# Fetching the slot lists and rows of all four early expert units during the fourth MLP block

## Chip, cores and metric

The kernel runs on one core of one Trainium2 chip. The metric is the device time of one execution in microseconds (us), lower is better; the number to predict is the median of several executions of the changed kernel. PE is TensorE, DVE is VectorE, ACT is ScalarE, POOL is GpSimd and SP is SyncE, which here only issues DMAs.

## What is computed

```python
attn = softmax((q @ k_m.T) / sqrt(64)) @ v_m      # k_m, v_m pooled by softmax(phi) over the sequence
x = elu(attn_out @ w_in) @ w_out                  # 2304 tokens, 512 -> 2048 -> 512
noisy = x @ w_gate + log1p(exp(x @ w_noise)) * noise
top2 = the two largest of the 8 experts for each token, with softmax weights top2_w
for e in range(8):
    for k in range(2):
        mask = top2[:, k] == e
        out[mask] += top2_w[mask, k, None] * (relu(x[mask] @ w1[e]) @ w2[e])   # 512 -> 1024 -> 512
```

## The kernel before

The work is one list of **units**, and each unit is a loop over slices of its hidden width (line 863 flattens both into iterations `i`). Units 0 to 3 are the four MLP blocks of 4, 5, 4 and 5 token tiles of 128, with 16 iterations each. Units 4 to 15 are experts, with 8 iterations each. Units 4 to 7 are the **early** units: the first 256 slots (two tiles) of experts 0 to 3, filled from the tokens of blocks 0 and 1 alone, so that they can run before the last block's tokens are routed. Units 8 to 11 are the other three tiles of the same experts, and units 12 to 15 are the other four experts with five tiles.

In an iteration PE runs `layer1` of its own slice (line 729) and `layer2` of the slice two iterations earlier (lines 775 to 777). ACT and DVE split fp32 weights into a high and a low part for iteration `i + 2` (lines 462 and 468), from a raw tile of 1 MB that serves two iterations; three raw tiles rotate (line 387), and each load (line 395) is issued seven iterations before its first slice, when its tile has just been freed.

An expert unit's tokens reach it in these steps:

- `gating(b)` runs after block `b` and ends in indirect scatters by POOL (line 634) that write each token's number and weight into its expert's slots of the DRAM table `lst`.
- `fetch(n)` reads the unit's slots of `lst` into the tile `ids` by a DMA on SP's queue (line 688), and then POOL gathers the rows, one tile `xg` of 128 rows by each indirect DMA (line 693). The gathers of early units read only rows of blocks 0 and 1 (line 685).
- `spread(n)` transposes each gathered tile on PE (line 704) and splits the result into `xh` and `xl` on ACT and DVE (lines 134 and 135). A unit's `spread` is queued when the unit ahead of it begins, and must be through when its own begins (`drain`, line 876).
- At a unit's end `put_rows` scales the accumulators and POOL adds them to `out` (line 797).

All engines take their instructions in the order in which the program was written down, so a waiting instruction holds everything behind it on its engine or queue. That order is set by two queues of generators, `heads` and `tails`, which `tick` advances at two or three places of every iteration. A generator that yields "next" goes on in the next iteration at the earliest. `fetch` yields four of these behind its gathers, so what stands behind it in `tails` comes four iterations later. Since `lst` is tracked as one DRAM tensor, a list read that stands behind a `gating`'s scatters in the program waits until they have landed.

Of the kernel before, what the change touches and what calls it, by code (L numbers as in the profile page):

```python
# [40 lines left out]
def moe_stack_kernel(ctx, tc, phi, kv, q, wmlp, wgn, noise, wmoe, out):  # L41
# [73 lines left out]
    def att_loads(b):  # L115
        return ([lambda: load_phi(b)] + [lambda w=w, c=c: load_kv(b, w, c) for w in range(2) for c in range(2)]
                + [lambda h=h: load_q(b, h) for h in range(2)])
# [9 lines left out]
    def settle():  # L127
        for f in deferred:
            f()
        deferred.clear()  # L130
# [277 lines left out]
    def fold(b, j, g):  # L408

        if g == 0:  # L410
            folds[b, j] = [fp.tile([P, 2, 512], F32R, tag=n, name=n) for n in ("fh", "fl")]
        bk = side_bank()
        for jj in range(2):
            pe.matmul(bk[64 * jj:64 * jj + 64], att["vT", b][:, g, 64 * jj:64 * jj + 64],
                      raws["a", 16 * b + 4 * j + 2 * g + jj], start=True, stop=True, tile_position=(0, 64 * jj))
        later(lambda: halve(bk, *(t[:, g] for t in folds[b, j])))
# [55 lines left out]
    heads, tails, moe = [], [], {}  # L472
    wants, stepped = {}, {}

    def step_on(gen):
        place[0] = ""
        wants[id(gen)] = next(gen)
# [28 lines left out]
    def drain(gen):  # L506
        place[0] = ""
        for queue in (heads, tails):
            while gen in queue:
                try:  # L510
                    next(queue[0])
                except StopIteration:
                    wants.pop(id(queue.pop(0)), None)
# [163 lines left out]
        yield  # L677


    def fetch(n, wait=0):  # L680

        for _ in range(wait):
            yield "next"
        mp = moe["pool"]
        rows = JUNK + (BLOCKS[2][0] * P if n["early"] else N)
        ids = mp.tile([P, 5, 2], I32, tag="ids", name="ids", bufs=6)
        a, nt = n["e"] * N + n["s0"], n["nt"]
        sp.dma_start(ids[:, :nt], lst[a:a + nt * P].rearrange("(t p) c -> p t c", p=P))
        n["ids"] = ids
        n["xg"] = []  # L690
        for tt in range(nt):
            xg = mp.tile([P, DM], F32, tag="xg", name="xg", bufs=12)
            pool.indirect_dma_start(out=xg, out_offset=None, in_=x2d[:rows],
                                    in_offset=bass.IndirectOffsetOnAxis(ap=ids[:, tt, 0:1], axis=0))
            n["xg"].append(xg)
        for _ in range(4):
            yield "next"

    def spread(n):
        xt = n["x"]  # L700
        for tt in range(n["nt"]):
            bk = side_bank()
            for c in range(4):
                pe.transpose(bk[:, c * P:(c + 1) * P], n["xg"][tt][:, c * P:(c + 1) * P], ident)
            v = bk.rearrange("p (c n) -> p c n", c=4)
            hi = xt[0][:, :, tt * P:(tt + 1) * P]
            later(lambda a=(v, hi, xt[1][:, :, tt * P:(tt + 1) * P]): halve(*a))
            yield

    def new_x():  # L710
        return [moe["pool"].tile([P, 4, 640], F32R, tag=n, name=n, bufs=2) for n in ("xh", "xl")]

    def splits(u):
        if u["kind"] == "mlp":
            return [(0, S // 2), (S // 2, S // 2)]
        n = u["nt"] * P
        return [(0, n)] if n <= 512 else [(0, n // 2), (n // 2, n // 2)]
# [41 lines left out]
    def hidden_c():  # L759
        for m, gh, gl, o in low:  # L760
            dve.tensor_tensor(gl[:, o], m, gh[:, o].bitcast(F32), op=OP.subtract)
        low.clear()
# [71 lines left out]
    k = NE * TPE + 1  # L834
# [4 lines left out]
    units = [dict(kind="mlp", blk=k, nt=BLOCKS[k][1], nf=16) for k in range(4)]  # L839
# [4 lines left out]
    late = 4 + NA  # L844
# [22 lines left out]
    for i in range(len(flat)):  # L867

        near = [flat[j][0]["nt"] for j in (i - LAG, i - LAG + 1) if 0 <= j < len(flat)]
        banks["tags"] = ["px"] + ["acc%d" % t for t in range(max(near, default=0), 5)]  # L870
        if i < len(flat):
            u, f = flat[i]
            k = units.index(u)
            if f == 0:
                if "need" in u:
                    drain(u["need"])
                if k == 1:
                    paced += zeros
                if k == 4:
                    moe["pair"] = True  # L880
                if k == 3:
                    side_stack.close()
                    moe["pool"] = ctx.enter_context(tc.tile_pool(name="moe", bufs=1))
                if k >= 3 and k + 1 < len(units):
                    n = units[k + 1]
                    n["x"] = new_x()
                    n["need"] = spread(n)
                    if k == 3:
                        tails += [fetch(n, 3), n["need"], fetch(units[5])]
                    else:  # L890
                        (heads if k + 1 in (late, late + 1) else tails).append(n["need"])
                        if k == late:
                            tails.append(overflow_table())
                        if k + 2 < len(units) and k + 2 not in (late, late + 1):
                            tails.append(fetch(units[k + 2]))
            if k in (1, 2) and f == 0:
                paced = att_loads(k + 1) + paced
            if k < 3 and f == 0:
                n = units[k + 1]
                n["need"] = attention(k + 1)  # L900
                heads.append(n["need"])
            if k and u["kind"] == "mlp" and f == 0:
                u["x"] = att["x", k]
            j = (i + 2) // 4
            turn_ = u["kind"] == "mlp" and f % 4 > 1 and j < 16
            if turn_:
                while ("vT", j // 4) not in att:
                    step_on(heads[0])
                place[0] = ""
                fold(j // 4, j % 4, f % 4 - 2)  # L910
            tick("", turn_)
            hidden_c()
            mine = [(h, c) for h, c in (("a", i + 5), ("b", i)) if c < NRAW]
            conv1_lo(mine)
            conv2(mine)
            nxt = []
            if u["kind"] == "mlp":
                nxt += [("b", i)] * (i >= NRAW)
            if 64 <= i + 2 < len(chunks):
                nxt += [("a", i + 2), ("b", i + 2)]  # L920
            prep_hi(nxt)
            gh = gp.tile([P, 640], F32R, tag="gh", name="gh")
            gl = gp.tile([P, 640], F32R, tag="gl", name="gl")
            cuts = splits(u)
            if u["kind"] == "mlp":
                elu, parts = ep.tile([P, 2, S], F32, tag="elu", name="elu"), []
            for j, (s0, n) in enumerate(cuts):
                ph = layer1(u, i, s0, n)
                if j == len(cuts) - 1:
                    tick("mid")  # L930
                o = slice(s0, s0 + n)
                if u["kind"] == "mlp":
                    elu_a(elu, ph, o)
                    parts.append((ph, o))
                else:
                    relu_(ph, gh, gl, o)
            settle()
            prep_lo(nxt)
            keep(mine)
            conv1_hi([(h, c) for h, c in (("a", i + 6), ("b", i + 1)) if c < NRAW])  # L940
            for n in at_end.get(i, []):
                load_to(n)
            for _ in range(2 if f < 10 else 1):
                if paced:
                    paced.pop(0)()
            if u["kind"] == "mlp":
                elu_b(u, f, elu, parts, gh, gl)
            tick("late")
            pend.append((u, f, i, gh, gl))
        else:  # L950
            tick()
        if i >= LAG and i < len(flat) - 1:
            pu, pf, pi, pgh, pgl = pend.pop(0)
            layer2(pu, pf, pi, pgh, pgl)
            if pf == pu["nf"] - 1:
                for t in range(pu["nt"]):
                    put_rows(pu, t, pu["acc"][t])
                if pu["kind"] == "mlp":
                    b = pu["blk"]
                    if b < 2:  # L960
                        tails.append(gating(b, pu["rows"]))
                    else:
                        heads.append(gating(b, pu["rows"]))
                    if b == 3:
                        heads += [fetch(units[late]), fetch(units[late + 1])]
# [70 lines left out]
```

## Time and profile before

| what | value |
|---|---|
| median of 3 executions | 962.58 us (962.42 to 963.52) |
| the profiled execution's own time | 955.79 us |
| its span in the profile | 954.0 us |
| PE busy / PE weight load busy | 898.1 us (94%) / 738.6 us (77%) |
| DVE, ACT, POOL busy | 549.6 us (58%), 452.1 us (47%), 173.5 us (18%) |
| mean granted clock of PE | 0.98 |
| moved by DMA | 153.11 MB, mean 160 GB/s |

Times in the trace count from the start of the span. The profiled execution is one sample beside the three that were timed; it is 6.79 us below their median. PE is the engine that is nearly always busy, so what matters of any other engine is whether PE has to wait for it. Block 3 ends at about 455 us, and the early units run their first layer from about 444 us to about 570 us: unit 4 from 444.7, unit 6 from 517.7 and unit 7 from 542.7 us.

### The profile page before, as it was taken

The numbers are of one execution on the slowest core, as the hardware profiler recorded it, in microseconds if no ns is written. First come the engines' busy times: TensorE is split into PE (matmuls) and PEld (weight loads), VectorE is DVE, ScalarE is ACT, GpSimd is POOL, SyncE is SP. The second block draws the span as 40 slices with busy tenths as digits, with TensorE's granted clock in tenths as the row PEclk, the third lists the DMA queues.
The fourth block names the chain that finished last, engine by engine and source line by source line (L and its number), as shares of the span: only waits on it lengthen the run. The fifth ranks groups of instructions, "written<-read, shape, count | busy, mean of one in ns | idle before, by whom it ended". The sixth has DMA issues, their size and how long they took to land. (4 is left out here: it accounts for less than half of the span.)

```text
span 954.0 us, 15080 instructions
## 1 busy us (share of the span) xinstructions
PE 898.1 (94%) x5688; PEld 738.6 (77%) x5690; DVE 549.6 (58%) x1199; ACT 452.1 (47%) x964; POOL 173.5 (18%) x281
## 2 busy tenths in 40 slices
PE   7699999999999989999985998999999999999995
PEld 4356457777778767768884987999999999999994
DVE  5888966566777685586662665545544352342321
ACT  4676546544565555456552553444444242332320
POOL 1000100000012233104054112204124023030303
PEclk9799999999999999999997999999999999999998
DMA  9897459554832325223627765457465236161404
GB/s 317 329 361 244 141 197 352 204 176 131 289 118 89 90 89 156 102 98 89 211 90 223 218 199 144 154 165 190 145 208 141 81 105 157 70 144 57 81 8 56
DMA packets 69612, 153.11 MB, mean 160 GB/s; under 512 B 11170, under 2 KB 20130, under 8 KB 69538
## 3 DMA queue, kind: packets, MB, share of 16 engines
q1 hardware_dynamic: 59426, 131.12, 40.9%
q0 software_dynamic: 10112, 21.02, 11.5%
q8 instruction: 45, 0.74, 0.3%
q14 instruction: 29, 0.24, 0.1%
HBM read 119.42 MB, written 32.69 MB: 159 GB/s over the span
## 5 line engine op out<-in xcount | busy, mean ns | idle before, releaser
L775 PE MATMUL acc<-bh,gl 128*128 128x512 f32 x544 | 218.9, 402 | 4.0 <-DVE rows L795 3.9
L776 PE MATMUL acc<-bl,gh 128*128 128x512 f32 x544 | 213.7, 393 | 0.0
L777 PE MATMUL acc<-bh,gh 128*128 128x512 f32 x544 | 213.6, 393 | 0.0
L757 DVE SCALAR_TENSOR_TENSOR gl<-ph,gh 128x320 fp32r<-128x320 f32 (+2 forms) x128 | 62.8, 491 | 228.4 <-ACT gh L756 228.4
L462 ACT ACTIVATE bh<-raw 128x512 fp32r<-128x512 f32 x144 | 90.0, 625 | 84.9 <-PE acc L777 84.2
L775 PEld LDWEIGHTS acc<-bh,gl 128*128 128x128 f32 x544 | 102.8, 189 | 23.6 <-DVE rows L795 4.9
L777 PEld LDWEIGHTS acc<-bh,gh 128*128 128x128 f32 x544 | 102.6, 189 | 23.0
L756 ACT ACTIVATE gh<-ph 128x320 fp32r<-128x320 f32 (+2 forms) x128 | 55.9, 437 | 134.5 <-PE ph L729 134.5
L776 PEld LDWEIGHTS acc<-bl,gh 128*128 128x128 f32 x544 | 102.9, 189 | 16.6
L797 POOL DMA_INDIRECT out<-rows,ids x40 | 65.3, 1632 | 276.7 <-DVE rows L795 268.7
L729 PE MATMUL ph<-xl,ah 128*128 128x320 f32 (+2 forms) x512 | 100.1, 318 | 0.0
L468 DVE TENSOR_TENSOR bl<-raw,bh 128x512 fp32r<-128x512 f32 x144 | 98.5, 684 | 2.9 <-ACT bh L462 2.9
L729 PE MATMUL ph<-xh,al 128*128 128x320 f32 (+2 forms) x512 | 97.1, 312 | 0.0
L729 PE MATMUL ph<-xh,ah 128*128 128x320 f32 (+2 forms) x512 | 97.0, 311 | 0.0
L729 PEld LDWEIGHTS ph<-xl,ah 128*128 128x128 f32 x512 | 84.0, 192 | 6.0 <-ACT bh L462 0.2
L729 PEld LDWEIGHTS ph<-xh,al 128*128 128x128 f32 x512 | 81.7, 191 | 0.0
L729 PEld LDWEIGHTS ph<-xh,ah 128*128 128x128 f32 x512 | 81.3, 190 | 0.0
L749 ACT ACTIVATE gh<-elu 128x576 fp32r<-128x576 f32 (+1 forms) x48 | 32.0, 667 | 101.7 <-DVE elu L743 101.7
L729 PEld LDWEIGHTS ph<-tl,fh 128*128 128x128 f32 x256 | 41.1, 191 | 40.8 <-issue 13.2
L729 PE MATMUL ph<-tl,fh 128*128 128x288 f32 x256 | 62.9, 327 | 10.2 <-DVE gh L743 5.3
L468 DVE TENSOR_TENSOR al<-raw,ah 128x512 fp32r<-128x512 f32 x96 | 65.5, 682 | 0.0
L734 ACT ACTIVATE elu<-ph 128x288 f32<-128x288 f32 x128 | 52.4, 409 | 23.7 <-PE ph L729 17.2
(218 smaller groups left out, 1272.6 us busy)
## 6 DMA issues: line engine op xcount, KB each, us to landing
raw<-in_wmoe SPq DMA_DIRECT2D x48, 1024.0 KB, 5.1
raw<-in_wmlp SPq DMA_DIRECT2D x32, 512.0 KB, 6.4
raw<-wxa SPq DMA_DIRECT2D x12, 1024.0 KB, 5.9
raw<-wxb SPq DMA_DIRECT2D x12, 1024.0 KB, 7.0
kv<-in_kv SPq DMA_DIRECT2D x8, 1024.0 KB, 11.9
out<-zrow SPq DMA_DIRECT2D x13, 512.0 KB, 8.7
q<-in_q SPq DMA_DIRECT2D x8, 576.0 KB, 9.2
x2d<-rows SPq DMA_DIRECT2D x18, 256.0 KB, 8.1
```

The source lines that it names most:

```text
L462: act.activation(ready[h, c][0], raws[h, c], AF.Copy)
L468: dve.tensor_tensor(lo, raws.pop((h, c)), hi.bitcast(F32), op=OP.subtract)
L729: pe.matmul(ph, w, x, start=k == 0, stop=k == len(terms) - 1)
L734: act.activation(t[:, 0, o], ph, AF.Exp)
L749: act.activation(gh[:, o], m, AF.Copy)
L756: act.activation(gh[:, o], ph, AF.Relu)
L757: dve.scalar_tensor_tensor(gl[:, o], ph, 0.0, gh[:, o].bitcast(F32), op0=OP.max, op1=OP.subtract)
L775: pe.matmul(acc, gl[:, o], wh, start=f == 0, stop=False)
L776: pe.matmul(acc, gh[:, o], wl, start=False, stop=False)
L777: pe.matmul(acc, gh[:, o], wh, start=False, stop=f == u["nf"] - 1)
L797: d = pool.indirect_dma_start(out=out, out_offset=bass.IndirectOffsetOnAxis(ap=ids[:, t, 0:1], axis=0), in_=r, in_offset=None, compute_op= ...
```

## The change

`fetch` gets a parameter for the number of iterations it lets pass behind its gathers. When unit 3 (the fourth block) begins, the fetches of units 4, 5, 6 and 7 are queued one behind the other, each one iteration after the one ahead, and the `spread` of unit 4 behind them all. Units 4 to 6 no longer queue a fetch; from unit 8 on it is as before.

```diff
-    def fetch(n, wait=0):
+    def fetch(n, wait=0, after=4):
...
-        for _ in range(4):
+        for _ in range(after):
             yield "next"
...
                     if k == 3:
-                        tails += [fetch(n, 3), n["need"], fetch(units[5])]
+                        tails += [fetch(n, 3, 1)] + [fetch(m, 0, 1) for m in units[5:late]] + [n["need"]]
                     else:
                         (heads if k + 1 in (late, late + 1) else tails).append(n["need"])
                         if k == late:
                             tails.append(overflow_table())
-                        if k + 2 < len(units) and k + 2 not in (late, late + 1):
+                        if late + 2 <= k + 2 < len(units):
                             tails.append(fetch(units[k + 2]))
```

**SP's queue while unit 5 runs.** `raw` are weight tiles from `in_wmoe`, `ids` slot lists: `ids_5481` is unit 7's, `ids_5584` unit 8's, `ids_5736` unit 9's. DMASW names a wait for an indirect DMA. Before:

```order
L395 DMA raw_5465<-in_wmoe 128x2x1024 [waits DMAHW1_49,DMAHW6_49,DVE_49,Activation_49]
L688 DMA ids_5481<-lst_89 128x2x2 [waits DMAHW2_49,DMASW1_49]
L395 DMA raw_5545<-in_wmoe 128x2x1024 [waits DMAHW3_49,DMAHW7_49,DVE_49,Activation_49]
L688 DMA ids_5584<-lst_89 128x3x2 [waits DMAHW4_49]
L395 DMA raw_5617<-in_wmoe 128x2x1024 [waits DMAHW0_49,DMAHW5_49,DVE_49,Activation_49]
L395 DMA raw_5681<-in_wmoe 128x2x1024 [waits DMAHW1_49,DVE_49,Activation_49]
L688 DMA ids_5736<-lst_89 128x3x2
```

With the change:

```order
L395 DMA raw_5471<-in_wmoe 128x2x1024 [waits DMAHW2_49,DMAHW7_49,DVE_49,Activation_49]
L395 DMA raw_5545<-in_wmoe 128x2x1024 [waits DMAHW0_49,DMAHW3_49,DVE_49,Activation_49]
L688 DMA ids_5584<-lst_89 128x3x2 [waits DMAHW4_49,DMASW3_49]
L395 DMA raw_5617<-in_wmoe 128x2x1024 [waits DMAHW1_49,DMAHW5_49,DVE_49,Activation_49]
L395 DMA raw_5681<-in_wmoe 128x2x1024 [waits DMAHW2_49,DMAHW6_49,DVE_49,Activation_49]
L688 DMA ids_5736<-lst_89 128x3x2
```

Unit 7's list is gone from here; the wait for the last scatters now stands at unit 8's list, one weight tile further on.

**POOL's queue, fourth block.** `xg` are the gathers, `g_rec` and `g_cum` belong to `gating(2)`. Before:

```order
L693 DMA xg_3970<-x2d_88,ids_3966 128x512
L693 DMA xg_4420<-x2d_88,ids_4418 128x512
L693 DMA xg_4422<-x2d_88,ids_4418 128x512
L557 COPY g_rec_4438<-tokid_97 128x4 x2
L583 COPY g_cum_4523<-run_103 128x8
L585 TENSOR_TENSOR g_cum_4523<-g_cum_4523,g_oh_4521 128x8 x3
```

With the change:

```order
L693 DMA xg_3970<-x2d_88,ids_3966 128x512
L693 DMA xg_4353<-x2d_88,ids_4351 128x512
L693 DMA xg_4355<-x2d_88,ids_4351 128x512
L693 DMA xg_4388<-x2d_88,ids_4386 128x512
L693 DMA xg_4390<-x2d_88,ids_4386 128x512
L557 COPY g_rec_4430<-tokid_97 128x4 x2
L693 DMA xg_4497<-x2d_88,ids_4495 128x512
L693 DMA xg_4499<-x2d_88,ids_4495 128x512
L583 COPY g_cum_4521<-run_103 128x8
```

Six gathers instead of two now stand ahead of the running count of `gating(2)`; the three lists they need (`ids_4351`, `ids_4386`, `ids_4495`) stand together on SP's queue in the same block.

**DVE, fourth block.** The split of unit 4's transposed rows (`xl<-px,xh`, two of them) moves down by three iterations, behind most of `gating(2)`. Its second new place, as the difference shows it:

```order
 L761 TENSOR_TENSOR gl<-elu,gh 128x576
 L761 TENSOR_TENSOR gl<-rest,gh 128x64
+L135 TENSOR_TENSOR xl<-px,xh 128x4x128
 L468 TENSOR_TENSOR bl<-raw,bh 128x512
 L742 SCALAR_TENSOR_TENSOR elu<-elu 128x288
 L743 SCALAR_TENSOR_TENSOR elu<-ph,elu 128x288
```

It now stands in front of the `elu` steps that free PE's `ph` bank; the transposes on PE and the first halves of the split on ACT move along with it. On PE nothing else changes its place: `spread` of units 5, 6 and 7 stands where it stood.

## Rows read from the trace of the kernel before

**Rows 1.** The page's first part: busy time, share, instructions of each engine.

```profile
PE 898.1 (94%) x5688; PEld 738.6 (77%) x5690; DVE 549.6 (58%) x1199; ACT 452.1 (47%) x964; POOL 173.5 (18%) x281
```

**Rows 2.** PE's waits: who waited for whom; us, times, longest.

```profile
PE acc L704 <- DMA xg<-x2d,ids: 11.4, 1, 11.4
```

**Rows 3.** PE's timeline, 495 to 545 us: start, duration, instruction, [idle before <-releaser].

```profile
504.91 0.39 PE L776 MATMUL acc<-bl,gh 128*128 128x512 f32 x1
505.14 0.40 PE L777 MATMUL acc<-bh,gh 128*128 128x512 f32 x1
516.96 1.09 PE L704 MATMUL acc<-ident,xg 128*128 128x128 f32 x4 [11.42 <-DMA xg<-x2d,ids]
...
520.76 0.48 PE L775 MATMUL acc<-bh,gl 128*128 128x512 f32 x1
...
542.36 0.60 PE L704 MATMUL acc<-ident,xg 128*128 128x128 f32 x4
542.72 0.72 PE L729 MATMUL ph<-xl,ah 128*128 128x256 f32 x4
...
544.59 0.48 PE L775 MATMUL acc<-bh,gl 128*128 128x512 f32 x1
```

**Rows 4.** Stretches: busy us (instructions) by engine, granted clock, DMA share, GB/s.

```profile
505.00:517.00 12.00, 0.58 (x4) 0.17 (x3) 1.27 (x3) 0.00 (x0) 4.82 (x5) 0.72 1.01 325
517.00:522.00 5.00, 5.00 (x25) 4.79 (x26) 1.44 (x3) 2.96 (x6) 0.93 (x1) 0.66 0.61 210
```

**Rows 5.** The timeline of SP's queue, 455 to 560 us.

```profile
464.60 24.83 SPq L395 DMA_DIRECT2D raw<-in_wmoe  x4
505.00 0.37 SPq L688 DMA_DIRECT2D ids<-lst  x1
505.53 0.38 SPq L395 DMA_DIRECT2D raw<-in_wmoe  x1
...
506.67 0.94 SPq L395 DMA_DIRECT2D raw<-in_wmoe  x2
```

**Rows 6.** The waits of SP's queue: us, times, longest.

```profile
SPq L688 <- DMA lst<-g_rec,g_slot: 29.0, 3, 15.5
```

**Rows 7.** POOL's timeline, 470 to 560 us.

```profile
499.55 1.27 POOL L634 DMA_INDIRECT lst<-g_rec,g_slot  x1 [0.23 <-issue]
...
510.37 1.01 POOL L693 DMA_INDIRECT xg<-x2d,ids  x1 [5.46 <-DMA ids<-lst]
...
521.07 0.95 POOL L693 DMA_INDIRECT xg<-x2d,ids  x1 [4.43 <-DMA ids<-lst]
```

**Rows 8.** Instructions that write or read raw weight tiles, 480 to 545 us.

```profile
DMA to landing us min/median/max: 4.8/6.0/12.3
```

**Rows 9.** DVE's timeline, 496 to 530 us, and ACT's, 488 to 530 us.

```profile
499.91 0.68 DVE L468 TENSOR_TENSOR bl<-raw,bh 128x512 fp32r<-128x512 f32 x1
...
525.85 0.62 ACT L462 ACTIVATE ah<-raw 128x512 fp32r<-128x512 f32 x1
```

**Rows 10.** All 40 gathers of line 693: duration in ns (min/median/max), first and last start.

```profile
L693 POOL DMA_INDIRECT xg<-x2d,ids x40: 941/971/1468, 374.2 to 795.9; - x40
...
DMA to landing us min/median/max: 3.3/5.1/7.8
```

**Rows 11.** SP's queue, 386 to 399 us, in the fourth block.

```profile
392.53 0.36 SPq L401 DMA_DIRECT2D raw<-wxa  x1
...
395.94 0.50 SPq L688 DMA_DIRECT2D ids<-lst  x1
```

**Rows 12.** POOL's timeline, 360 to 470 us.

```profile
402.05 1.19 POOL L693 DMA_INDIRECT xg<-x2d,ids  x1 [25.22 <-DMA ids<-lst]
...
419.94 0.75 POOL L585 TENSOR_TENSOR g_cum<-g_cum,g_oh 128x8 bf16<-128x8 bf16 x3 [15.01 <-DVE g_e L588]
```

**Rows 13.** DVE's and PE's timelines, 396 to 432 us.

```profile
401.13 0.69 DVE L135 TENSOR_TENSOR xl<-px,xh 128x512 fp32r<-128x512 f32 x1 [2.26 <-ACT xh L134]
...
424.22 0.50 PE L729 MATMUL ph<-tl,fh 128*128 128x288 f32 x2 [1.02 <-DVE elu L743]
```

## The prediction

> **What bounds the kernel now.** I read four views in this order: the page's first part, PE's waits, the timelines around the longest of these, and the queues that it points to. The first part says that PE works 94% of the span [rows 1]. So an edit that moves fetches can only pay if PE waits for one of them. PE's waits answer that at once: the longest single stop of the whole span is one wait of 11.4 us for a gather, at the transposes of line 704 [rows 2].
>
> PE's timeline shows where. PE starts a last matmul of unit 5 at 505.14 us and then nothing until the transposes at 516.96 us [rows 3]. These belong to the `spread` of unit 7, which stands in the first iteration of unit 6, a whole unit ahead of its use; but PE takes its instructions in order, so all of unit 6 stands behind them. In this stretch PE has four instructions, and its granted clock has fallen as well: 0.72 as a mean of 505 to 517 us and still 0.66 from 517 to 522 us [rows 4]. After a stop, part of the work is done at 1.2 instead of 2.4 GHz.
>
> Why is the gather late? Follow it back. POOL starts it at 510.37 us, released by the slot list, and the list was issued on SP at 505.00 us [rows 5, 7]. SP issued its previous DMA at 464.60 + 24.83 = 489.4 us and then stood still for 15.5 us, the longest of three waits for the scatters into `lst` [rows 5, 6]. The last of those, from `gating(3)`, starts on POOL at 499.55 us [rows 7]. Unit 7 takes slots that the last block never fills, so it waits for writes that do not concern it, only because its list read stands behind them in the program. The stop in full: last scatter 499.55, list issued 505.0, gather 510.4, rows landed just before 517.0.
>
> **The change, part by part.**
>
> *The stop of unit 7 goes.* Its list and gathers now stand in the fourth block, a hundred us earlier, ahead of the scatters of `gating(2)` and `gating(3)`. Its last two matmuls start 0.23 us apart (504.91 and 505.14), so without the stop the transposes would start at 505.14 + 0.23 = 505.37 us, not 516.96: **11.6 us** (the wait's own row says 11.42, because it counts from a modelled end) [rows 3].
>
> *So does the slow work behind it.* From the transposes to the first `layer2` matmul of that iteration PE takes 516.96 to 520.76 = 3.80 us. The same pieces, two transposed tiles around one `layer1`, take 542.36 to 544.59 = 2.23 us one unit later at full clock [rows 3]. **1.6 us** more.
>
> *Unit 6's fetch moves too*, at no gain: PE waits at line 704 only once [rows 2], and that is unit 7's. Of SP's 29.0 us in waits for scatters [rows 6] one falls away, which no weight tile needed.
>
> *Three lists and six gathers in the fourth block.* Unit 5's list is issued at 395.94 us now; with the change it goes out behind the raw tile of 392.53 us, and those of units 6 and 7 at about 396 and 396.5 us [rows 11]. Today the gather behind the list of 395.94 starts at 402.05 us [rows 12], 6.1 us later. So two gathers start at about 399, two at 402 and two at 405 us; at 0.97 us each [rows 10], POOL is through by about 408 us. What is queued behind them is the running count of `gating(2)`, which waits for DVE until 419.94 us anyway [rows 12]. Some 12 us of cover: **0**.
>
> *Unit 4's `spread` moves down three iterations.* PE's transposes are as many as before. On DVE each split takes 0.69 us [rows 13]. It now stands ahead of the `elu` steps for which PE already waits 1.02 us at 424.22 us [rows 13]. PE has four transposes more to do in that time, 542.36 to 542.72 = 0.36 us by their like in unit 7 [rows 3], so the wait grows by about 0.69 - 0.36 = 0.33 us. Ends: -0.5, if DVE's relief three iterations earlier shortens another such wait; +1.4, if both splits count in full (2 x 0.69). I take **+0.3**, nearest to the row of the wait.
>
> *The wait for the last scatters goes to unit 8's list.* SP still stops until 505.0 us, now with weight tile 5617 behind it instead of 5545. DVE has freed its buffer at 499.91 + 0.68 = 500.6 us [rows 9], so the tile goes out at 505.4, 4.8 us late. ACT wants it when it splits the weights for iteration 84; that was 525.85 us [rows 9], and with 13.2 us less it is 512.6. The median landing of these tiles is 6.0 us, the shortest 4.8 [rows 8]: 510.2 to 511.4. It just fits, **0**; the longest landing, 12.3 us, came when three tiles and five gathers went out together [rows 4, 5, 8].
>
> Sum: -11.6 - 1.6 + 0.3 = -12.9 us. Against the profiled execution (955.79 us) that makes 942.9 us. The three timed runs have a median 6.79 us above it, and I see nothing in the trace that scales with the edit, so I take the same difference from the median: 962.58 - 12.9 = **949.7 us**.
>
> **The rivals.**
>
> *Weights late.* If tile 5617 takes the longest landing, 505.4 + 12.3 = 517.7 us, ACT is held up, and behind it the relu that frees `ph`. PE wants that bank in iteration 84. Iterations 80 and 88 begin with the transposes of units 7 and 8, at 505.4 and 529.2 us once the stop is gone (542.36 - 13.2), 2.98 us apart each, so iteration 84 begins at about 517.3 us. From the landing to the free bank I estimate 2 us: two splits at 0.62 on ACT [rows 9], and the relu on ACT and DVE. PE waits 517.7 + 2.0 - 517.3 = 2.4 us, and I add the 1.6 us of slow clock that followed the long stop, though a short one may do without: 953.7 us. For it: SP really is stopped there. Against: two tiles now go out where three did. The cost starts where the landing passes 10 us.
>
> *POOL late in the fourth block.* One of today's two gathers there took 1.19 us against a median of 0.97; the longest of all 40 is 1.47 us [rows 10, 12]. At 1.47 each, six gathers end at about 411 us, still 9 us ahead of the count. Each would have to last 2 us longer before PE felt it at the `gating(2)` matmuls; if it does, I put 3 us on it: 952.7 us. The Trainium skill ("SBUF — State Buffer", section "SBUF: two separate sides") has a rule by which this could be so: while DVE runs an operation that takes the port it shares with GpSimd, descriptors of DMAs issued from GpSimd cannot be written, and it gives 620 ns alone against 3100 ns overlapped. By that, as an estimate, the six gathers would last 15 us longer and end near 423 us, 3 us late. The 1.19 us row shows a fifth of a microsecond, not two and a half.
>
> *The stop moves to unit 8.* Its list is now the first behind the scatters. Its transposes came at 542.36 us and come at 529.2 us now; its gathers start at about 510.4 us as unit 7's did, three of them end near 514, and the longest landing of any gather is 7.8 us [rows 3, 7, 10]: 522 us, 7 us to spare. Past 529 us every microsecond costs one, and past 542 us the change is a loss. That takes a further wait like the 15.5 us one [rows 6] and a longest landing of the list on top: 505 + 15.5 + 12.3 + 3.8 + 7.8 = 544.4 us, a stop of 15.2 us and 1.6 us of clock, 966.5 us. Unit 9's gathers, behind two weight tiles, started at 521.07 us [rows 7], which speaks against it.
>
> *The stop stays.* If the gathers, not the list, were what waits for something of `gating(3)`, nothing changes: 962.6 us. The release by the list at 510.37 [rows 7] speaks against it.
>
> **How the numbers follow.** The forecast gets 0.78, weights late 0.10, POOL late 0.04, the stop at unit 8 0.04, the stop that stays 0.04. The range runs from the forecast with the good end of the fourth block and one slow-clock stretch more or less, 949.7 - 0.8 - 1.6 = 947.3, rounded out to 946.5, to weights late with part of the bad end of the fourth block, 953.7 + 0.8 = 954.5. A difference of 0.2% is 1.9 us, about what can be told from no change. Faster: 0.78 + 0.10 + 0.04 = 0.92; same 0.04; slower 0.04.
>
> **What would show it.** PE's waits hold no wait of line 704 for a gather; the first iteration of unit 6 follows unit 5 without a gap and the clock stays at 1.0 there; SP's longest wait for `lst` stands at unit 8's list, near 505 us; six gathers start between 398 and 408 us; the count of `gating(2)` still ends its wait by DVE; the wait at 424 us grows by tenths. I am wrong if PE waits more than 2 us at unit 8's transposes or at weights around 510 to 520 us.

## The result and the profile after

The changed kernel takes 950.13 us (median of 4, 947.23 to 951.39) against 962.50 us (4 runs, 961.69 to 963.52): a ratio of 0.9872, 95% interval 0.9852 to 0.9891, 12.4 us less. 949.7 was forecast. The profiled execution took 947.23 us, with a span of 945.5 us.

The first part of the page, answering [rows 1]:

```profile
PE 895.4 (95%) x5688; PEld 734.6 (78%) x5690; DVE 549.8 (58%) x1199; ACT 450.7 (48%) x964; POOL 171.7 (18%) x281
```

PE's waits, answering [rows 2] (who waits for whom; us in total, times, longest):

```profile
PE ph L729 <- DVE gh L743: 5.7, 3, 5.2
PE acc L775 <- DVE rows L795: 3.7, 2, 3.4
...
PE px L704 <- DVE fl L135: 1.4, 1, 1.4
```

PE does the same 5688 instructions. The wait of 11.4 us for a gather is gone; no wait for a gather at line 704 is left. Two small ones for DVE are new at that line, the one shown and one of 1.18 us at 451.48 us. PE's timeline where unit 7's transposes stand now (start, duration, instruction, idle before and releaser), answering [rows 3]:

```profile
508.87 0.40 PE L777 MATMUL acc<-bh,gh 128*128 128x512 f32 x1
509.10 0.60 PE L704 MATMUL acc<-ident,xg 128*128 128x128 f32 x4
509.98 0.74 PE L729 MATMUL ph<-xl,ah 128*128 128x256 f32 x4 [0.29 <-DVE gl L757]
...
511.99 0.48 PE L775 MATMUL acc<-bh,gl 128*128 128x512 f32 x1
```

From unit 5's last matmul to the first `layer2` matmul of unit 6, PE took 520.76 - 505.14 = 15.62 us before and takes 511.99 - 508.87 = 3.12 us now. The stretches of [rows 4] (busy us and instructions of PE, PEld, DVE, ACT and POOL; then clock, DMA share, GB/s):

```profile
505.00:517.00 12.00, 11.71 (x76) 10.31 (x75) 8.96 (x17) 7.25 (x16) 3.28 (x4) 1.00 0.92 139
517.00:522.00 5.00, 4.97 (x32) 4.27 (x31) 2.54 (x6) 2.90 (x7) 2.93 (x3) 1.00 1.03 395
```

76 PE instructions where there were 4, and the granted clock is 1.00, the 2.4 GHz level, throughout. The wait for the scatters is still on SP, now at unit 8's list. From the waits of SP's queue, answering [rows 6]:

```profile
SPq L688 <- DMA lst<-g_rec,g_slot: 19.6, 2, 12.6
```

and its timeline, answering [rows 5]:

```profile
486.55 12.54 SPq L395 DMA_DIRECT2D raw<-in_wmoe  x3
511.77 0.37 SPq L688 DMA_DIRECT2D ids<-lst  x1
512.30 0.90 SPq L395 DMA_DIRECT2D raw<-in_wmoe  x2
```

SP stands still from 499.1 to 511.8 us, and it no longer matters: between 512 and 537 us PE's timeline has no wait at all.

The span fell by 954.0 - 945.5 = 8.5 us only, while the medians lie 12.4 apart. Set side by side by one DVE step of each iteration (line 742 in the blocks, line 757 in the experts), the changed kernel's profiled execution is 0.9 us ahead up to iteration 40, 1.4 us behind in iteration 49 and 3.9 to 4.0 us behind in iterations 51 to 54, at 373.9 to 392.4 us; the first moved instruction comes at 396.87 us. Both parts of that lag, 2.2 us that start near 311 us and 2.5 us near 365 us, come with stops for which the trace shows no releaser. The timeline of all engines near 365 us, in the changed kernel:

```profile
363.24 0.96 POOL L634 DMA_INDIRECT lst<-g_rec,g_slot  x1 [0.23 <-issue]
...
364.82 0.69 DVE L135 TENSOR_TENSOR fl<-px,fh 128x512 fp32r<-128x512 f32 x1 [3.60 <-issue]
...
365.57 0.66 PE L533 MATMUL px<-ident,rows 128*128 128x128 f32 x4 [2.10 <-issue]
...
367.85 0.41 ACT L734 ACTIVATE elu<-ph 128x288 f32<-128x288 f32 x1 [2.54 <-remote]
```

So an execution that is a few microseconds slow ahead of the change is compared with one that is not. From iteration 75 to 84, around the edit's place, the same comparison gives 3.7 us behind and then 8.8 us ahead, 12.5 us.

### The profile page after: what moved, and what is told of

It reads as the page before. It is cut to its first block, busy times and chain, and to the rows that moved or that the text cites. A ratio compares the mean times of both kernels' runs of the same rounds, so it can differ in the third digit from the quotient of the medians.

```text
span 945.5 us, 15083 instructions
## 1 busy us (share of the span) xinstructions
PE 895.4 (95%) x5688; PEld 734.6 (78%) x5690; DVE 549.8 (58%) x1199; ACT 450.7 (48%) x964; POOL 171.7 (18%) x281
```

## The experiments

**Theory**: PE, bound to its order, stood still because unit 7's list read stood behind scatters that do not concern it; moving that one fetch is the gain, and the rest of the edit is worth tenths. **Rivals**: the spread of the work over the fourth block is what pays; the weight tile behind the moved wait takes a part back; the gathers crowd the fourth block.

Four kernels ran on one chip, where the kernel before has a median of 961.05 us (17 runs), and four on another, where it has 954.63 us (11 runs). Ratios are to the kernel before on the same chip.

### Unit 7's fetch alone

From the kernel before, only unit 7's fetch goes into the fourth block:

```diff
-                        tails += [fetch(n, 3), n["need"], fetch(units[5])]
+                        tails += [fetch(n, 3), n["need"], fetch(units[5]), fetch(units[7])]
...
-                        if k + 2 < len(units) and k + 2 not in (late, late + 1):
+                        if k + 2 < len(units) and k + 2 not in (late - 1, late, late + 1):
```

> Unit 7's list and rows take the place that unit 6's had, and unit 6's go a few iterations later but still ahead of the last scatters; units 4 and 5 stay as before. Theory (the whole gain is the list read of unit 7 that stood behind the last scatters): the stop of 11.4 us is gone, 949.5 us, within 2 us of the change, no wait of line 704 for a gather. Rival (fetching in the fourth block, with SP and POOL free later, is worth something by itself): 2 us or more slower than the change.

Measured: 949.18 us, ratio 0.9871 (0.9836 to 0.9906), the whole gain of the change. PE's timeline at the place:

```profile
509.31 0.39 PE L777 MATMUL acc<-bh,gh 128*128 128x512 f32 x1
509.54 0.60 PE L704 MATMUL acc<-ident,xg 128*128 128x128 f32 x4
...
512.22 0.48 PE L775 MATMUL acc<-bh,gl 128*128 128x512 f32 x1
```

2.91 us where the kernel before took 15.62. One list and two gathers carry the result. They need not stand as early as in the change: here SP stood still for 20.4 us in front of unit 7's list, for the scatters of `gating(2)`, and issued it at 450.09 us, and PE's timeline has no wait that follows from it. The longest wait for the scatters on SP, and the list:

```profile
SPq L688 <- DMA lst<-g_rec,g_slot: 40.6, 3, 20.4
...
450.09 0.37 SPq L688 DMA_DIRECT2D ids<-lst  x1
```

What counts is that the list stands ahead of the scatters of `gating(3)`.

### Everything but unit 7

From the change, unit 7's fetch goes back behind the scatters; units 4 to 6 stay as the change has them:

```diff
-                        tails += [fetch(n, 3, 1)] + [fetch(m, 0, 1) for m in units[5:late]] + [n["need"]]
+                        tails += [fetch(n, 3, 1)] + [fetch(units[5], 0, 1), fetch(units[6], 0, 2), n["need"]]
...
-                        if late + 2 <= k + 2 < len(units):
+                        if k + 2 == late - 1 or late + 2 <= k + 2 < len(units):
```

> As the change, but unit 7's fetch stays where it was; units 5 and 6 are fetched in the fourth block and unit 4's transposes move down. Theory: nothing is gained, 962.5 us or up to 1.2 us more, and the stop of about 11 us at line 704 stands where it stood. Rival (the number of lists and gathers in the early units is what makes the gather late): a clearly shorter stop and at least 3 us gained.

Measured: 961.33 us (12 runs), ratio 0.9991 (0.9966 to 1.0015): nothing is left of the gain, and the stop is back. Its wait among PE's waits:

```profile
PE acc L704 <- DMA xg<-x2d,ids: 7.9, 1, 7.9
```

It reads 7.9 instead of 11.4 us because other stops, without a releaser, had already held PE back on the way there: this profile is 8.9 us behind the kernel before in the iteration ahead of the transposes and 6.1 us in the one behind them. Such a wait absorbs what was lost before it. The two kernels together say that unit 7's fetch is enough and is needed.

### The late gather kept, only PE's transposes moved

From the kernel before, the list stays late, but unit 7's `spread` is queued five iterations later, so that unit 6's matmuls stand ahead of it:

```diff
-    def spread(n):
-        xt = n["x"]
+    def spread(n, wait=0):
+        xt = (yield from ["next"] * wait) or n["x"]
...
-                    n["need"] = spread(n)
+                    n["need"] = spread(n, 5 if k + 1 == late - 1 else 0)
```

> All fetches as before; only unit 7's transposes come five iterations later. Theory (PE stopped because its transposes stood a unit ahead of their use, and the late list also held weight tiles back): the 11.4 us wait at line 704 is gone, but weight tiles that go out at 505.5 us instead of about 495 us now stop PE for 2 to 3 us around iteration 82: 951.5 to 953.5 us. Rival A (weights never matter): 949.5 us, as the change. Rival B (the weights would have stopped PE for as long as the gather did): 960 us or more.

Measured: 954.22 us, ratio 0.9909 (0.9876 to 0.9942), a little more than expected. The wait at line 704 for a gather is gone, so most of the stop was PE's order, not a want of rows. But 5.0 us are missing against unit 7's fetch alone (949.18 on the same chip). Part of it is the weight tile that SP held back, on ACT's timeline:

```profile
519.76 0.63 ACT L462 ACTIVATE ah<-raw 128x512 fp32r<-128x512 f32 x1 [4.56 <-DMA raw<-in_wmoe]
```

and PE's timeline around it:

```profile
508.47 0.74 PE L729 MATMUL ph<-xl,ah 128*128 128x256 f32 x4 [1.43 <-issue]
...
525.09 0.50 PE L775 MATMUL acc<-bh,gl 128*128 128x512 f32 x1 [1.59 <-DVE rows L795]
```

The 1.59 us follow from the late tile: DVE waits 4.08 us for ACT and then works without a pause up to the `rows` step for which PE waits, which its timeline shows:

```profile
521.22 0.43 DVE L757 SCALAR_TENSOR_TENSOR gl<-ph,gh 128x256 fp32r<-128x256 f32 x1 [4.08 <-ACT gh L756]
...
524.29 0.74 DVE L795 TENSOR_SCALAR rows<-acc,ids 128x512 f32<-128x512 f32 x1
```

The 1.43 us have no releaser. Set beside the kernel before by the start of PE's first `layer1` matmul of each iteration, this profile falls 3.2 us behind on the way to iteration 79, where stops like that one stand, and 1.8 us around the wait of 1.59 us; the profile of unit 7's fetch alone loses nothing at the first place. So in this one execution the late weight tile reached PE and cost 1.8 us. How the 5.0 us between the medians divide is not shown.

### Unit 4 first

From the change, unit 4's fetch and `spread` keep their old place, and the other three fetches follow:

```diff
-                        tails += [fetch(n, 3, 1)] + [fetch(m, 0, 1) for m in units[5:late]] + [n["need"]]
+                        tails += [fetch(n, 3), n["need"]] + [fetch(m, 0, 1) for m in units[5:late]]
```

> As the change, but unit 4's transposes stay where they were, ahead of the lists of units 5, 6 and 7. Theory (the move of unit 4's transposes behind most of the gating costs 0.3 to 1.2 us): 0 to 1.2 us below the change, 949 to 950 us, and the waits of line 704 for DVE in the fourth block are gone. Rival (that move is free or gains): equal to the change or above it.

Measured: 952.96 us (949.19 to 956.78), ratio 0.9895 (0.9858 to 0.9932), above what was expected, but its interval takes in that of the change: undecided by time. In its profile PE no longer waits at line 704 in the fourth block, but has the waits for `elu` of the kernel before again (1.35 us at 426.39 and 1.02 us at 432.83 us). And PE lost 2.19 us elsewhere, behind a stop of ACT's that names a PE instruction long done (the last `layer2` matmul ends at 508.7 us):

```profile
510.03 0.38 ACT L756 ACTIVATE gh<-ph 128x256 fp32r<-128x256 f32 x1 [5.11 <-PE acc L777]
```

Nothing of the edit stands there. What unit 4's move is worth is read from PE's timelines below, and they speak against the theory of this run.

### The change again, and unit 8's list later

On the second chip ran the change unaltered, and the change with unit 8's list four iterations later, so that SP issues its weight tiles first:

```diff
-                        heads += [fetch(units[late]), fetch(units[late + 1])]
+                        heads += [fetch(units[late], 4, 1), fetch(units[late + 1])]
```

> The change itself, once more, beside the next three on one chip: 12 to 13 us below the kernel before (ratio 0.987), with a spread of 3 to 4 us between executions as in the first four runs.

> As the change, but unit 8's list is read four iterations later, when the last scatters should have landed, so that SP does not stand still ahead of weight tile 84. Theory (that tile is late but PE does not feel it): the same time as the change within 1 us, while SP's longest wait for the scatters falls from 12.6 us to under 3 us and ACT's waits for raw tiles (1.7 and 0.9 us) go. Rival (late weights cost PE time in the change): 1.5 to 4 us below it.

Measured: 942.13 us, ratio 0.9871 (0.9844 to 0.9897), for the change, the same ratio at another level, with executions from 940.82 to 946.22 us; and 942.36 us, 0.9863 (0.9837 to 0.9889), with the list later. In the profile of the unaltered change PE's timeline has no wait from 505 to 537 us, and the place reads as the prediction drew it:

```profile
504.54 0.40 PE L777 MATMUL acc<-bh,gh 128*128 128x512 f32 x1
504.77 0.60 PE L704 MATMUL acc<-ident,xg 128*128 128x128 f32 x4
505.13 0.72 PE L729 MATMUL ph<-xl,ah 128*128 128x256 f32 x4
...
506.99 0.47 PE L775 MATMUL acc<-bh,gl 128*128 128x512 f32 x1
```

506.99 - 504.54 = 2.45 us, 15.62 - 2.45 = 13.17 us less. ACT's timeline has two waits for weights:

```profile
514.12 0.63 ACT L462 ACTIVATE ah<-raw 128x512 fp32r<-128x512 f32 x1 [1.96 <-DMA raw<-in_wmoe]
...
518.39 0.63 ACT L462 ACTIVATE ah<-raw 128x512 fp32r<-128x512 f32 x1 [1.53 <-DMA raw<-in_wmoe]
```

With the list later ACT has no wait for these tiles, SP's longest wait for the scatters is 5.7 us (more than expected), and the time is the same. So a lateness of up to 1.96 us at ACT cost nothing in the change.

### The overflow table later

One of the next stops in PE's waits is 3.4 us for `rows`, at line 775, after the end of unit 7, where the first `layer2` of unit 8 needs a bank that unit 7's result still holds; the kernel before has it too, at 580.66 us. DVE computes `overflow_table` there, 24 small operations in two goes, ahead of the `rows` step that frees PE's bank. In the profile of the change on this chip, DVE's last operation of the table and the `rows` step behind it, and PE's stop:

```profile
566.15 0.18 DVE L674 CAST o_tab<-o_res 1x64 int32<-1x64 f32 x1
566.26 0.73 DVE L795 TENSOR_SCALAR rows<-acc,ids 128x512 f32<-128x512 f32 x1
```

```profile
562.75 0.86 PE L729 MATMUL ph<-xh,ah 128*128 128x384 f32 x4
567.05 0.50 PE L775 MATMUL acc<-bh,gl 128*128 128x512 f32 x1 [3.43 <-DVE rows L795]
```

From the change, the table goes behind the next fetch:

```diff
-                        if k == late:
-                            tails.append(overflow_table())
                         if late + 2 <= k + 2 < len(units):
                             tails.append(fetch(units[k + 2]))
+                        if k == late:
+                            tails.append(overflow_table())
```

> As the change, but the overflow table is queued behind unit 10's fetch, so its small DVE steps leave the place where unit 7's rows are taken out of the accumulators. Theory (the next longest stop of PE, 3.4 us for line 795 at about 572 us, comes from these DVE steps standing ahead of it, and half-speed work follows): that stop goes and 3.5 to 5 us are gained over the change. Rival (the stop is the accumulators' own turn-over, or the steps only stop PE elsewhere): under 1 us.

Measured: 938.36 us, ratio 0.9825 (0.9798 to 0.9851), 3.8 us below the change on the same chip. Two stretches in the profile of the change (busy us of the engines as above):

```profile
562.00:567.00 5.00, 1.61 (x10) 1.30 (x8) 4.72 (x15) 2.29 (x5) 0.00 (x0) 1.00 0.48 137
567.00:570.00 3.00, 2.95 (x8) 2.37 (x9) 1.66 (x3) 0.00 (x0) 2.47 (x3) 0.59 0.66 145
```

The same stretches, and one more, with the table later:

```profile
562.00:567.00 5.00, 5.00 (x27) 4.46 (x26) 3.71 (x7) 2.93 (x6) 4.17 (x6) 1.00 0.56 169
567.00:570.00 3.00, 3.00 (x17) 2.85 (x16) 0.60 (x2) 1.28 (x3) 2.03 (x3) 1.00 0.99 350
...
575.00:580.00 5.00, 5.00 (x28) 4.56 (x27) 4.45 (x21) 1.98 (x4) 0.00 (x0) 1.00 0.24 94
```

The table's work now stands at 575.7 to 582.6 us, beside a PE that stays busy. PE at the place of the old stop:

```profile
564.23 0.86 PE L729 MATMUL ph<-xh,ah 128*128 128x384 f32 x4
564.93 0.40 PE L775 MATMUL acc<-bh,gl 128*128 128x512 f32 x1
```

From the last `layer1` group to `layer2` PE takes 564.93 - 564.23 = 0.70 us, where the change takes 567.05 - 562.75 = 4.30 us: 3.6 us less. By DVE's steps of each iteration the kernel gains 5.3 us there on the change, so about 1.7 us are work at the lower clock behind the stop.

### Both

> Both edits together. Theory: the sum of the two, 3.5 to 5 us below the change, 944 to 947 us where the kernel before takes 962. Rival (they act on the same slack): no more than the better of the two.

With both edits: 937.87 us (935.83 to 938.21), ratio 0.9815 (0.9792 to 0.9838). That is 4.3 us below the change on the same chip, as expected; the absolute 944 to 947 us were reckoned from the other chip's level. The 0.5 us to the table alone lie within the runs, as the list's move alone gave nothing. It is the fastest version run, 16.8 us below the kernel before.

## Why the prediction was right

*The stop and the slow work behind it, -11.6 and -1.6.* Right, in place, mechanism and size. The profile with no other disturbance gives 13.17 us, against a forecast of 13.2. That unit 7's fetch alone is the cause was argued ahead from the chain of list, gather and transposes and is now shown from both sides: with it alone 0.9871, with all but it 0.9991.

*Unit 6's fetch at no gain.* Right: the kernel without unit 7's fetch has moved unit 6's, and gains nothing.

*Three lists and six gathers at nothing.* Right. POOL's timeline of the changed kernel, answering [rows 12]:

```profile
402.96 1.26 POOL L693 DMA_INDIRECT xg<-x2d,ids  x1 [26.01 <-DMA ids<-lst]
...
410.40 0.95 POOL L693 DMA_INDIRECT xg<-x2d,ids  x1 [0.31 <-issue]
...
421.22 0.75 POOL L585 TENSOR_TENSOR g_cum<-g_cum,g_oh 128x8 bf16<-128x8 bf16 x3 [9.67 <-DVE g_e L588]
```

The count still waits 9.67 us for DVE. The gathers started some 4 us later than forecast, as that execution was 3.9 us behind; on the second chip they start at 398.99 to 406.36 us. The rival of a late POOL fell: the six lasted 946 to 1263 ns, 1538 at most on the second chip, with DVE busy for 7.0 of the 10 us. The rule of the Trainium skill that was named for it ("SBUF — State Buffer", section "SBUF: two separate sides"), by which descriptors stand still while DVE holds the shared port, had no effect of its size here; the page ties it to certain DVE operations, and no run here varied these.

*Unit 4's `spread`, +0.3.* This step failed, in place and in sign. I expected a wait of PE's for `elu` to grow; that wait of 1.02 us [rows 13], and one of 1.34 us an iteration ahead of it, are gone, and in their stead PE waits 1.40 us at the transposes themselves, which now stand behind DVE's work of `gating(2)`:

```profile
422.65 0.66 PE L704 MATMUL px<-ident,xg 128*128 128x128 f32 x4 [1.40 <-DVE fl L135]
```

That is 1.34 + 1.02 - 1.40 = 0.96 us less waiting, and most of it is kept. The same two `layer1` matmuls on both sides of the stretch, in the kernel before and then in the change on the second chip:

```profile
392.42 0.53 PE L729 MATMUL ph<-tl,fh 128*128 128x288 f32 x2
...
439.32 0.42 PE L729 MATMUL ph<-tl,fh 128*128 128x288 f32 x2
```

```profile
392.31 0.53 PE L729 MATMUL ph<-tl,fh 128*128 128x288 f32 x2
...
438.58 0.42 PE L729 MATMUL ph<-tl,fh 128*128 128x288 f32 x2
```

46.90 us before and 46.27 us with the change, a gain of 0.6 us where a loss of 0.3 was forecast. The first profile of the change has 46.28 us, and "Unit 4 first", which leaves the transposes in place, 46.91 us. So the good end of my working, -0.5 (DVE's relief shortens another such wait), was the right one, and the rival of that run (the move is free or gains) holds by these profiles; the medians can't tell it.

*The wait moves to unit 8's list, 0.* Right, but closer than the forecast's "just fits": the weights came late for ACT, by 1.69 and 0.85 us in one profile and by 1.96 and 1.53 us in the other, and PE felt nothing. The rival's working fits too: it put the tile's landing 5.1 us behind ACT's time and PE's wait at 2.4 us, so 2.7 us of lateness were to be free. Up to 1.96 us cost nothing, and the 4.56 us in the third experiment, where the order is another, came with a wait of 1.59 us on PE.

*The stop moves to unit 8.* It did not. Its gathers began at 517.20 to 525.84 us, and its transposes started at 533.55 us without a wait.

*From the profile to the median.* I took the difference of one profiled execution to the median as constant, 6.79 us. For the change it is 950.13 - 947.23 = 2.9 us, so this step failed. The sum in its own terms would have put the profiled execution at 942.9; it took 947.23, in good part for the lag that it had ahead of the edit. That the forecast of the median came within 0.4 us is in part luck: unit 4's term was 0.9 us off, and from iteration 55 to the end the second chip's profile gains 13.5 us on the kernel before, where the medians fell by 12.4 and 12.5. Why the medians gained less is not shown; only one execution of each kernel is traced.

## What to carry to other kernels

Where engines take their instructions in program order, look for the instruction that waits for something it does not need, and for what is queued behind it: here a list read waited for scatters into other rows of the same tensor, and a whole unit of matmuls waited behind two transposes for the next unit. Price such a stop as the gap plus the slow-clock work behind it, and take the wait that inherits the delay to its own consumer before charging it. After the longest stop is gone, read the list of waits again: one of the next gave another 0.4% for two lines moved.

## What the runs showed of the hardware

On the two chips the same kernel took 961.05 and 954.63 us, 0.7% apart and more than many edits are worth, yet the change has the ratios 0.9872 and 0.9871.

In the profiles of the change and of the four experiments of the first set, engines stop for up to 5.9 us without a releaser, near 311 to 319 us, near 365 us, in some near 447 us, and near 500 to 512 us, each time while or just after POOL issues scatters of line 634. Further such stops of ACT and DVE come later, from 530 us on, where no scatter of that line runs. The profiles of the second set and of the kernel before, which issue the same scatters, lack all of these, so the scatters alone are not the cause; it stays open, and no run was made for it. In the profile of the change the first two places cost 2.2 and 2.5 us, together over a third of what the change gains. Whether they account for the difference between the chips, or for the 6.79 us between the kernel before's profile and its median, is not shown.

A stop of 3.43 us was followed by 3 us at a mean granted clock of 0.59, so that the lower level, 1.2 GHz, ruled most of it; behind the stop of 11.4 us the clock was 0.66 over 5 us [rows 4]. The price behind the short stop, about 1.7 us, was no smaller than the 1.6 us behind the long one. And the same waits do not bring the lower level each time. PE waits twice for 1.0 us in `gating(3)`, at 478 and 479 us in the kernel before and at 483 and 484 us in the first profile of the change. The stretches around them, before and with the change:

```profile
476.00:486.00 10.00, 7.88 (x44) 6.91 (x43) 7.05 (x25) 4.69 (x10) 1.02 (x5) 0.83 0.34 124
481.00:491.00 10.00, 7.89 (x52) 6.73 (x51) 8.15 (x29) 5.66 (x12) 1.41 (x8) 1.00 0.37 126
```

The clock is 0.83 in one and 1.00 in the other, and by the iterations the second gains 1.5 us there though no edit touches the place. A single profile carries such differences into its span.
